# Attention, then eight experts on one core: a few steps of the hand-over moved, and the experts' order table written anew

## The chip, the cores and the metric

The kernel runs on one core of a Trainium2 chip. The metric is the device time of one execution in microseconds (us). The runs of the kernel before gave 601.39, 601.55 and 603.48 us; the median, 601.55 us, is what the change is held against.

## What is computed

The first half is attention in two steps for 8 batches, 8 heads, 576 tokens: 32 packed queries `p` attend to `k` and `v`, and the tokens' queries `q` attend to the 32 packed rows. Its result `x` (4608 x 512) goes to 8 experts. Each expert takes exactly 576 tokens, in the order of all router logits:

```
p_packed = sm_attn(p, k, v);  x = sm_attn(q, p_packed, p_packed)
order = argsort(-(x @ w_gate).flatten())
for idx in order:                      # token, expert
    if assigned[tok] >= 0 or counts[e] >= cap: continue
    assigned[tok] = e; counts[e] += 1
for e in range(E):
    out[assigned == e] = relu(x[assigned == e] @ w1[e]) @ w2[e]
```

All values are float32. The kernel splits each operand of the expert products into a high part and a low part and multiplies three of the four pairs.

## The kernel before, in words

**Attention** is worked through in 16 groups (half the heads of one batch each). A table, `ORDER` (one list per engine, lines 51 to 96), names every step in the order in which its engine gets it, and `follow` (line 271) issues them so. `x0` to `x4` are five TensorE products per group that make rows of `x` (line 715), `xe0` to `xe4` copy them from PSUM to SBUF (lines 742 and 744), and `x_st` (lines 746 to 752) stores them to `xd` in HBM with three DMAs. Those of the last group, 15, go two by SP's queue and one by ACT's. The same table holds the choice of the first expert's tokens, which no loop searches for: `pick_b` finds the expert and marks its tokens, `which` (`expert(0)`, line 1195) turns the expert's number into an integer, and `slot_a` to `slot_f`, `onehot`, `slot_v` and `list_m` to `list_b` (lines 1229 to 1291) number the marked tokens and make the list of their rows. `slot_a` counts the marked tokens by a TensorE product, `slot_b` copies the count, `slot_c` adds two products, the second of which reads that copy. Nine products with zeros (`warm`) stand behind `slot_c`.

**The experts** follow another table, `PACE` (from line 110 on): 2083 steps in one list, and each engine gets its own steps in the list's order. For expert `k`: `gather.k.c` (POOL, line 1302) fetches its 576 rows from `xd` in five pieces; experts 0 and 1 turn them by TensorE (`xt_p`, line 1335, then `xt_h` on ACT, line 1341, and `xt_l` on VectorE, line 1346), the others by way of HBM and VectorE (`xg_st`, `xg_ld`, `xt_t`, `xs_h`, `xs_l`). `load.k.q.w` fetches quarter `q` of weight 1 or 2 (512 KB, SP's queue, lines 1359 and 1363), `split_h` makes its high part on ACT (line 1368) and `split_l` the low part on POOL (line 1374, four pieces each; VectorE for the two of quarter 0 of expert 0). `f1.k.f.n.i` are TensorE's products for the hidden rows (line 1390; `n` is the half of the tokens, `i` the pair of parts), `h_hi` and `h_lo` (ACT line 1396, VectorE line 1401) empty their PSUM bank, `f2.k.f.t` are the products of the second layer (lines 1410 to 1415), `ev` and `ev_b` empty them, and `scatter` (POOL, line 1446) writes the rows out. A load into a buffer waits for the split that read it before.

Beside expert `k` runs the search for the tokens of expert `k+1` and later: `close`, `build` (lines 1052 to 1086, `build_b` is lines 1065 and 1066), then rounds of `count_a` (ACT, line 1098), `count_v` (VectorE, line 1104), `count_m` (TensorE, lines 1110 and 1111) and `upd`, and at last `slot` and `list` as above. `count_a`, `xt_h`, `h_hi`, `split_h` and `ev` share ACT's queue; `slot_e` (lines 1250 to 1252), `build_b`, `h_lo`, `xt_t` and `xs_l` share VectorE's. Three PSUM banks, in turn, serve `f1` and all the small products.

The first expert starts with 24 products with zeros (`warm.0.i`, line 416), spread over the wait for the first gathers. `held_m` (line 1021), `lim_t` and `lim_m` are small products that the search needs before its first round. Two loads of the first expert are held back (`HELD`, line 1348): ahead of the load, SP issues a 4-byte DMA from the tile that a gather fills (`hold`, line 1355), and so SP's queue waits there until that gather has landed.

Of the kernel before, what the change touches and what calls it, by code (L numbers as in the profile page):

```python
# [108 lines left out]

PACE = '''  # L110
    warm.0.0 lead.0 load.0.0.2 warm.0.1 load.0.0.1 warm.0.2 gather.0.0 warm.0.3 warm.0.4 warm.0.5 load.0.1.1 gather.0.1 held_m.0 lim_t.0 held_b.0 warm.0.6 warm.0.7 gather.0.2 lim_b.0
    warm.0.8 split_h.0.0.2 close_a.1 warm.0.9 close_b.1 lim_m.0 gather.0.3 warm.0.10 build_a.1 lim_c.0 warm.0.11 warm.0.12 warm.0.13 split_h.0.0.1 gather.0.4 warm.0.14 build_b.1
    warm.0.15 warm.0.16 warm.0.17 build_s.1 build_t.1 warm.0.18 build_v.1 warm.0.19 warm.0.20 count_v.1.0 warm.0.21 count_a.1.0 xt_p.0.0 split_l.0.0.1 warm.0.22 xt_h.0.0 load.0.1.2
    count_m.1.0 xt_p.0.1 upd_a.1.0 xt_l.0.0 xt_h.0.1 xt_p.0.2 upd_b.1.0 warm.0.23 xt_l.0.1 xt_h.0.2 f1.0.0.0.0 count_a.1.1 xt_l.0.2 load.0.2.1 f1.0.0.0.1 count_v.1.1 f1.0.0.0.2
    upd_c.1.1 count_m.1.1 xt_p.0.3 h_hi.0.0.0 upd_a.1.1 h_lo.0.0.0 xt_p.0.4 xt_h.0.3 upd_b.1.1 xt_h.0.4 f1.0.1.0.0 xt_l.0.3 count_a.1.2 f1.0.1.0.1 xt_l.0.4 f1.0.1.0.2 upd_c.1.2
    f1.0.0.1.0 count_v.1.2 h_hi.0.1.0 split_h.0.1.1 f1.0.0.1.1 h_lo.0.1.0 split_l.0.0.2 f1.0.0.1.2 count_m.1.2 split_l.0.1.1 f1.0.2.0.0 h_hi.0.0.1 split_h.0.1.2 h_lo.0.0.1 f1.0.2.0.1
    load.0.2.2 upd_a.1.2 f2.0.0.3 upd_b.1.2 upd_c.1.3 count_a.1.3 count_v.1.3 f1.0.1.1.0 build_k.1 f1.0.1.1.1 split_h.0.2.1 split_l.0.1.2 load.0.3.1 f1.0.1.1.2 count_m.1.3 f2.0.0.4
    h_hi.0.1.1 upd_a.1.3 f1.0.2.0.2 upd_b.1.3 h_lo.0.1.1 count_a.1.4 f2.0.0.1 count_v.1.4 upd_c.1.4 f1.0.2.1.0 split_l.0.2.1 split_h.0.2.2 load.0.3.2 count_m.1.4 f2.0.1.4 upd_a.1.4
    upd_b.1.4 f2.0.0.0 h_hi.0.2.0 upd_c.1.5 count_a.1.5 h_lo.0.2.0 f2.0.1.1 count_v.1.5 f1.0.2.1.1 f1.0.3.0.0 split_l.0.2.2 count_m.1.5 f1.0.2.1.2 upd_a.1.5 upd_b.1.5 f2.0.1.3
    count_v.1.6 h_hi.0.2.1 count_a.1.6 h_lo.0.2.1 f2.0.0.2 upd_c.1.6 f1.0.3.1.0 split_h.0.3.1 count_m.1.6 f1.0.3.1.1 upd_a.1.6 upd_b.1.6 f1.0.3.0.1 upd_c.1.7 count_a.1.7 split_l.0.3.1  # L120
    f1.0.3.0.2 count_v.1.7 f2.0.1.2 h_hi.0.3.0 split_h.0.3.2 count_m.1.7 f2.0.1.0 upd_a.1.7 upd_b.1.7 h_lo.0.3.0 f2.0.2.2 count_a.1.8 count_v.1.8 split_l.0.3.2 f1.0.3.1.2 upd_c.1.8
    f1.0.4.0.0 h_hi.0.3.1 count_m.1.8 f1.0.4.0.1 upd_a.1.8 upd_b.1.8 f1.0.4.0.2 h_lo.0.3.1 bound_m.1 f2.0.2.0 h_hi.0.4.0 bound_a.1 bound.1 test_c.1 f2.0.2.1 h_lo.0.4.0 test_m.1
    f1.0.4.1.0 test_t.1 test_k.1 f2.0.3.0 assign.1 f1.0.4.1.1 member.1 expert.1 close_a.2 load.1.0.1 slot_a.1 f1.0.4.1.2 close_b.2 f2.0.3.2 h_hi.0.4.1 slot_b.1 build_a.2 f1.0.5.0.0
    load.1.0.2 slot_c.1 f1.0.5.0.1 load.1.1.1 build_b.2 f2.0.2.3 load.1.1.2 slot_d.1 build_s.2 slot_e.1 build_t.2 f1.0.5.0.2 build_v.2 f2.0.3.3 h_lo.0.4.1 count_a.2.0 slot_f.1 f2.0.2.4
    count_v.2.0 f2.0.3.1 onehot.1 h_hi.0.5.0 split_h.1.0.1 count_m.2.0 f1.0.5.1.0 upd_a.2.0 upd_b.2.0 f2.0.4.2 slot_v.1 count_a.2.1 split_l.1.0.1 f2.0.4.0 h_lo.0.5.0 count_v.2.1
    f1.0.5.1.1 split_h.1.0.2 upd_c.2.1 list_m.1 count_m.2.1 f1.0.5.1.2 list_a.1 upd_a.2.1 split_l.1.0.2 f2.0.4.3 upd_b.2.1 load.1.2.1 h_hi.0.5.1 upd_c.2.2 count_a.2.2 h_lo.0.5.1
    list_s.1 f1.0.6.0.0 count_v.2.2 f2.0.5.0 list_b.1 split_h.1.1.1 count_m.2.2 f2.0.3.4 upd_a.2.2 upd_b.2.2 f1.0.6.0.1 gather.1.0 load.1.2.2 count_v.2.3 count_a.2.3 f1.0.6.1.0
    upd_c.2.3 build_k.2 f1.0.6.0.2 gather.1.1 split_h.1.1.2 f1.0.6.1.1 count_m.2.3 f2.0.4.1 upd_a.2.3 h_hi.0.6.0 split_l.1.1.1 upd_b.2.3 f2.0.5.3 upd_c.2.4 count_a.2.4 h_lo.0.6.0
    f1.0.6.1.2 count_v.2.4 f1.0.7.0.0 h_hi.0.6.1 split_h.1.2.1 count_m.2.4 f1.0.7.0.1 h_lo.0.6.1 upd_a.2.4 f1.0.7.0.2 gather.1.2 upd_b.2.4 load.1.3.1 count_v.2.5 count_a.2.5 f2.0.5.1
    upd_c.2.5 f2.0.4.4 gather.1.3 split_h.1.2.2 f2.0.5.2 count_m.2.5 f1.0.7.1.0 h_hi.0.7.0 gather.1.4 upd_a.2.5 upd_b.2.5 f1.0.7.1.1 h_lo.0.7.0 count_a.2.6 upd_c.2.6 xt_p.1.0  # L130
    count_v.2.6 split_l.1.2.1 f1.0.7.1.2 xt_h.1.0 f2.0.5.4 h_hi.0.7.1 count_m.2.6 f2.0.6.0 upd_a.2.6 h_lo.0.7.1 f2.0.6.2 upd_b.2.6 count_v.2.7 count_a.2.7 f2.0.7.0 xt_l.1.0
    split_l.1.1.2 xt_p.1.1 upd_c.2.7 xt_p.1.2 xt_h.1.1 count_m.2.7 f2.0.6.1 xt_h.1.2 upd_a.2.7 upd_b.2.7 xt_l.1.1 xt_p.1.3 count_a.2.8 f2.0.6.4 upd_c.2.8 load.1.3.2 f2.0.7.4
    count_v.2.8 xt_h.1.3 xt_p.1.4 xt_l.1.2 f2.0.6.3 xt_h.1.4 xt_l.1.3 ev.0.0 count_m.2.8 f2.0.7.1 upd_a.2.8 xt_l.1.4 split_h.1.3.1 scatter.0.0 f1.1.0.0.0 upd_b.2.8 count_v.2.9
    f1.1.0.0.1 count_a.2.9 upd_c.2.9 f1.1.0.1.0 split_l.1.2.2 f1.1.0.1.1 ev.0.4 count_m.2.9 f1.1.0.0.2 upd_a.2.9 upd_b.2.9 f1.1.0.1.2 count_v.2.10 h_hi.1.0.0 count_a.2.10 f2.0.7.3
    h_lo.1.0.0 upd_c.2.10 split_l.1.3.1 f2.0.7.2 ev_b.0 ev.0.3 count_m.2.10 f1.1.1.0.0 h_hi.1.0.1 upd_a.2.10 upd_b.2.10 ev.0.1 f1.1.1.0.1 h_lo.1.0.1 ev.0.2 bound_m.2 f1.1.1.0.2
# [1633 lines left out]
```

## Time and profile before

| what | value |
|---|---|
| median of the runs | 601.55 us |
| the profiled execution's own time | 600.76 us |
| its span, first to last instruction | 599.0 us |
| attention and the first expert's list | 0 to about 140 us |
| first product of the first expert | 149.82 us |
| TensorE busy | 580.4 us (97% of the span) |
| VectorE, ScalarE, GpSimd busy | 399.0, 341.8, 369.1 us |

The span is 1.76 us shorter than the profiled execution's time, which is 0.79 us under the median. Times in the rows count from the span's start. A matmul's end in the profile is modelled; the distance from one start to the next is the better measure of what a product costs. "Idle" before an instruction is the time in which its engine did nothing, and the name behind the arrow is what ended it.

### The profile page before, as it was taken

The page shows a single profiled execution, that of the slowest core. Times are in us where ns is not written, and L with a number is a line of the kernel's source. Part 1 is how long each engine was busy: PE and PEld are TensorE (multiplying, and loading weights), DVE is VectorE, ACT ScalarE, POOL GpSimd, SP SyncE. Part 2 cuts the span into 40 slices and gives each one's busy share as a digit, 9 for nine tenths or more (in the row PEclk, how much of TensorE's full clock was granted, in tenths as well). Part 3 has the DMA queues.
Part 4 walks back from the last instruction along what each step waited for, and adds up shares of the span by engine and source line. Part 5 has one row for each costly group of instructions (what it writes and reads, how often), then busy time and mean ns, then how long its engine had stood idle before and what let it go on. Part 6 is the DMA issues. An engine that isn't in the chain of part 4 may idle for free.

```text
span 599.0 us, 12421 instructions
## 1 busy us (share of the span) xinstructions
PE 580.4 (97%) x4145; PEld 494.3 (83%) x4145; DVE 399.0 (67%) x1438; ACT 341.8 (57%) x873; POOL 369.1 (62%) x617
## 2 busy tenths in 40 slices
PE   7999999997999999999999999999999999999994
PEld 4678888784888888887988888989888899989883
DVE  6999999987868685697588649756954342162110
ACT  4888889873857847656655573674443352342111
POOL 6589898883556768548844783881578467453003
PEclk9999999999999999999999999999999999999998
...
GB/s 291 391 370 261 307 333 231 192 159 225 170 10 242 123 164 208 220 91 166 249 130 113 149 242 131 150 197 182 53 203 210 239 78 196 212 8 80 1 1 84
DMA packets 75307, 105.76 MB, mean 177 GB/s; under 512 B 7124, under 2 KB 54756, under 8 KB 75236
## 3 DMA queue, kind: packets, MB, share of 16 engines
...
q8 instruction: 35, 0.57, 0.4%
q10 hardware_dynamic: 576, 0.34, 0.2%
...
## 4 chain that ended last, share of the span: by engine, by line
PE 87%; DVE 5%; ACT 2%; POOL 2%; issue 1%; DMA 1%; SPq 0%; POOLq 0%; DVEq 0%; ACTq 0%
PE hp L1390 34%; PE y L1410 10%; PE y L1411 10%; PE y L1412 9%; PE s L530 9%; PE xp L715 4%; PE y L1414 3%; PE y L1415 2%; PE pp L589 1%; DMA kl<-in_k_dram 1%; PE tr L574 1%; PE pl L1273 1%; PE px L1335 1%; ACT ja L1098 1%; POOL sb L653 1%
## 5 line engine op out<-in xcount | busy, mean ns | idle before, releaser
L1401 DVE SCALAR_TENSOR_TENSOR h<-hp,h 128x64 fp32r<-128x64 f32 (+3 forms) x192 | 61.8, 352 | 107.4 <-ACT h L1396 106.7
L1396 ACT ACTIVATE h<-hp 128x288 fp32r<-128x288 f32 (+2 forms) x128 | 51.7, 407 | 134.0 <-PE hp L1390 65.9
L1374 POOL TENSOR_TENSOR w1l<-w1s,w1h 128x256 fp32r<-128x256 f32 x124 | 89.7, 754 | 53.4 <-ACT w1h L1368 53.2
L1374 POOL TENSOR_TENSOR w2l<-w2s,w2h 128x256 fp32r<-128x256 f32 x124 | 90.5, 761 | 47.2 <-ACT w2h L1368 47.1
L1410 PE MATMUL y<-w2h,h 128*128 128x512 f32 x256 | 103.8, 406 | 0.0
L1411 PE MATMUL y<-w2l,h 128*128 128x512 f32 x256 | 100.6, 393 | 0.0
L1412 PE MATMUL y<-w2h,h 128*128 128x512 f32 x256 | 100.2, 391 | 0.0
L1390 PE MATMUL hp<-xh,w1h 128*128 128x288 f32 (+2 forms) x512 | 89.7, 298 | 1.0 <-DVE h L1401 0.9
L1390 PE MATMUL hp<-xh,w1l 128*128 128x288 f32 (+2 forms) x512 | 90.1, 299 | 0.0
L1390 PE MATMUL hp<-xl,w1h 128*128 128x288 f32 (+2 forms) x512 | 89.8, 298 | 0.0
L1390 PEld LDWEIGHTS hp<-xh,w1h 128*128 128x128 f32 x512 | 77.8, 188 | 7.4 <-ACT h L1396 1.1
L1446 POOL DMA_INDIRECT out_dram<-xg,gi x40 | 39.3, 983 | 69.7 <-DVE xg L1433 35.7
L1098 ACT ACTIVATE ja<-Vt,nT 128x288 bf16<-128x288 f32 x116 | 62.2, 536 | 32.7 <-DVE nT L1125 24.7
L1390 PEld LDWEIGHTS hp<-xl,w1h 128*128 128x128 f32 x512 | 76.4, 188 | 3.5 <-DVE xl L1346 0.2
L1390 PEld LDWEIGHTS hp<-xh,w1l 128*128 128x128 f32 x512 | 76.0, 188 | 2.9
L1412 PEld LDWEIGHTS y<-w2h,h 128*128 128x128 f32 x256 | 48.1, 188 | 10.8
L1302 POOL DMA_INDIRECT xg<-xd,gi x40 | 38.2, 955 | 23.1 <-issue 9.2
L1410 PEld LDWEIGHTS y<-w2h,h 128*128 128x128 f32 x256 | 48.1, 188 | 4.8
L1411 PEld LDWEIGHTS y<-w2l,h 128*128 128x128 f32 x256 | 48.2, 188 | 4.5
L1116 DVE SCALAR_TENSOR_TENSOR g<-pc,thr,s4r 128x3 f32<-128x3 f32 x64 | 14.0, 219 | 41.2 <-PE pc L1111 40.9
L1368 ACT CAST w2h<-w2s 128x1024 fp32r<-128x1024 f32 x32 | 33.3, 1042 | 13.1 <-DMA w2s<-in_moe_w_dram 6.7
L715 PE MATMUL xp<-P,th 128*128 128x264 f32 (+2 forms) x160 | 38.2, 328 | 0.7 <-DVE xs L742 0.3
...
## 6 DMA issues: line engine op xcount, KB each, us to landing
w2s<-in_moe_w_dram SPq DMA_DIRECT2D x32, 512.0 KB, 3.7
w1s<-in_moe_w_dram SPq DMA_DIRECT2D x32, 512.0 KB, 4.4
...
```

Source lines behind the costliest of these rows:

```text
L530: nc.tensor.matmul(t[:, 224 + 9 * a:224 + 9 * b], w[:, db].rearrange("p a b -> p (a b)"), x[:, :, db, a:b].rearrange("p b (t y) -> p t b y ...
L715: nc.tensor.matmul(xp[:m, :n], T[a, g][:, o:o + m], T[w, g][:, :n], start=i == 0, stop=i == 2)
L1098: nc.scalar.activation(ja, Vf, AF.Sign, bias=S_['nT'][:, j:j + 1], scale=-1.0, accum_out=cp[:, j:j + 1])
L1302: nc.gpsimd.indirect_dma_start(out=X['xg', k, c][:m], out_offset=None, in_=xd, in_offset=bass.IndirectOffsetOnAxis(ap=X['gi', k][:m, c:c + ...
L1374: eng.tensor_sub(X[n + 'l', k, q][r], X[n + 's', k, q][r], X[n + 'h', k, q][r].bitcast(F32))
L1390: nc.tensor.matmul(X['hp', k, f, n], X[W, k, q][:, d, 128 * r:128 * r + 128], X[Z, k][:, d, cut(k) * n:576 * n + cut(k) * (1 - n)], start= ...
L1396: nc.scalar.activation(X['h', k, f][:, cut(k) * n:576 * n + cut(k) * (1 - n)], X['hp', k, f, n], AF.Relu)
L1401: V.scalar_tensor_tensor(h[:, o:o + b - a], p[:, a - t * n:b - t * n], 0.0, h[:, a:b].bitcast(F32), op0=OP.max, op1=OP.subtract)
L1410: nc.tensor.matmul(y, hh, wh, start=f == 0, stop=False)
L1411: nc.tensor.matmul(y, hh, wl, start=False, stop=False)
L1412: nc.tensor.matmul(y, hl, wh, start=False, stop=f == 7)
L1446: s = nc.gpsimd.indirect_dma_start(out=out, out_offset=bass.IndirectOffsetOnAxis(ap=X['gi', k][:m, t:t + 1], axis=0), in_=X['yo', k, t][:m ...
```

## The change

Five edits of the code. `slot_a` moves ahead of `x4.15`, the last product of `x`. `which` moves from ACT to VectorE, behind `pick_b`. The third store of group 15 goes by ACT's queue, not SP's. The first expert's load (quarter 1, weight 1) is held until gather 1 has landed; before, it was the one behind it. `PACE` is a new list of the same 2083 steps.

```diff
 ORDER 'ACT':  -  keep_c xe4.14 xe0.15 xe1.15 xe2.15 xe3.15 xe4.15 which
               +  keep_c xe4.14 xe0.15 xe1.15 xe2.15 xe3.15 xe4.15
 ORDER 'DVE':  -  ... choice2 choice3 pick_b slot_b held_a slot_d ...
               +  ... choice2 choice3 pick_b which slot_b held_a slot_d ...
 ORDER 'PE':   -  x3.15 x4.15 slot_a slot_c warm list_m list_s
               +  x3.15 slot_a x4.15 slot_c warm list_m list_s
 PACE = '''
-    warm.0.0 lead.0 load.0.0.2 warm.0.1 load.0.0.1 warm.0.2 gather.0.0 warm.0.3 warm.0.4 warm.0.5 load.0.1.1 gather.0.1 held_m.0 lim_t.0 held_b.0 ...
+    warm.0.0 lead.0 load.0.0.2 warm.0.1 load.0.0.1 warm.0.2 warm.0.3 warm.0.4 held_m.0 warm.0.5 held_b.0 lim_t.0 warm.0.6 gather.0.0 ...
...
     def x_st(g):
...
         for i in range(2):
             q = nc.scalar if g == 15 and i else nc.sync
             q.dma_start(...)
-        nc.sync.dma_start(bass.AP(tensor=xd.tensor, ...), xs[lanes(g, 4), 4, :256])
+        q.dma_start(bass.AP(tensor=xd.tensor, ...), xs[lanes(g, 4), 4, :256])
...
-                ... ('which', 'ACT', .2, lambda: expert(0, nc.scalar), [('pick_b',)]),
+                ... ('which', 'DVE', .2, lambda: expert(0), [('pick_b',)]),
...
-    HELD = {(0, 1, 2): 1, (0, 2, 1): 4}
+    HELD = {(0, 1, 1): 1, (0, 2, 1): 4}
```

A line is one further down in the changed kernel, from the tables on. Three places are shown.

TensorE, end of attention. L715 are the products of `x` (here `x4.15`, three of them), L1231 is `slot_a`, L1239 and L1240 are `slot_c`. Before:

```order
L715 MATMUL xp<-P_2170,th 128x256
L715 MATMUL xp<-P_2301,th 128x256
L715 MATMUL xp<-P_2170,tl 128x256
L1231 LDWEIGHTS mb
L1231 MATMUL psl<-one,mb 36x1
L1239 LDWEIGHTS tri
L1239 MATMUL psl_2429<-mb,tri 128x36
L1240 LDWEIGHTS cs
L1240 MATMUL psl_2429<-tri,cs 128x36
```

Now:

```order
L1232 LDWEIGHTS mb
L1232 MATMUL psl<-one,mb 36x1
L716 MATMUL xp<-P_2170,th 128x256
L716 MATMUL xp<-P_2301,th 128x256
L716 MATMUL xp<-P_2170,tl 128x256
L1240 LDWEIGHTS tri
L1240 MATMUL psl_2429<-mb,tri 128x36
L1241 LDWEIGHTS cs
L1241 MATMUL psl_2429<-tri,cs 128x36
```

`slot_a` stands ahead of `x4.15`'s three products, `slot_c` behind them as before. Not shown, in the new table: five products with zeros instead of six stand ahead of `held_m`, and two stand between the transposes `xt_p.0.1` and `xt_p.0.2`, which followed each other. On ACT, `split_h.0.1.1` now comes ahead of `h_hi.0.1.0` and `count_a.1.2`.

SP's queue from the last store on. L752 (now L753) is the third store, the TENSOR_LOAD reads the first expert's number into a register, w2s and w1s are loads of weights, `hold` is the 4-byte DMA. Before:

```order
L752 DMA xd<-xs 64x256
L1352 TENSOR_LOAD ei
L1352 ISA x2
L1363 ISA
L1363 DMA w2s<-in_moe_w_dram 128x2x512
L1359 ISA
L1359 DMA w1s<-in_moe_w_dram 128x4x256
L1359 ISA
L1359 DMA w1s<-in_moe_w_dram 128x4x256
L1355 DMA hold<-xg 1x1
L1363 ISA
L1363 DMA w2s<-in_moe_w_dram 128x2x512
```

Now:

```order
L752 DMA xd<-xs 64x4x256
L1353 TENSOR_LOAD ei
L1353 ISA x2
L1364 ISA
L1364 DMA w2s<-in_moe_w_dram 128x2x512
L1360 ISA
L1360 DMA w1s<-in_moe_w_dram 128x4x256
L1356 DMA hold<-xg 1x1
L1360 ISA
L1360 DMA w1s<-in_moe_w_dram 128x4x256
L1364 ISA
L1364 DMA w2s<-in_moe_w_dram 128x2x512
```

The third store is gone from this queue, and `hold` stands ahead of the third load instead of the fourth.

POOL, boundary of experts 1 and 2, from the second scatter of expert 1 on. The DMAs to out_dram are scatters of expert 1, L1374 (now L1375) are low parts of weights: w2l is `split_l.2.3.2`, w1l is `split_l.2.3.1`. Before:

```order
L1445 MEMSET spc 1x1
L1446 DMA out_dram<-xg,gi 4608x512
L1374 TENSOR_TENSOR w2l<-w2s,w2h 128x256 x4
L1445 MEMSET spc 1x1
L1446 DMA out_dram<-xg,gi 4608x512
L1445 MEMSET spc 1x1
L1446 DMA out_dram<-xg,gi 4608x512
L1445 MEMSET spc 1x1
L1446 DMA out_dram<-xg,gi 4608x512
L1374 TENSOR_TENSOR w1l<-w1s,w1h 128x256 x4
```

Now:

```order
L1446 MEMSET spc 1x1
L1447 DMA out_dram<-xg,gi 4608x512
L1446 MEMSET spc 1x1
L1447 DMA out_dram<-xg,gi 4608x512
L1446 MEMSET spc 1x1
L1447 DMA out_dram<-xg,gi 4608x512
L1446 MEMSET spc 1x1
L1447 DMA out_dram<-xg,gi 4608x512
L1375 TENSOR_TENSOR w2l<-w2s,w2h 128x256 x4
L1375 TENSOR_TENSOR w1l<-w1s,w1h 128x256 x4
```

`split_l.2.3.2` moves from behind the second of the five scatters to behind all of them. In the table, `slot_e.3` and `build_b.4` stand ahead of it now. At the next boundary `split_l.3.3.2` moves the other way, ahead of all scatters of expert 2, and `slot_e.4` stands 25 steps behind it rather than right behind it.

## Rows read from the trace of the kernel before

**Rows 1.** The page, head and part 1: busy time, share of the span, instructions

```profile
span 599.0 us, 12421 instructions
PE 580.4 (97%) x4145; PEld 494.3 (83%) x4145; DVE 399.0 (67%) x1438; ACT 341.8 (57%) x873; POOL 369.1 (62%) x617
```

**Rows 2.** Windows, PE: stretch, length, PE busy, clock, DMA share, GB/s

```profile
254.00:308.00 54.00, 53.02 (x347) 1.00 0.57 167
308.00:362.00 54.00, 53.16 (x337) 1.00 0.58 164
362.00:416.00 54.00, 54.00 (x348) 1.00 0.54 169
```

**Rows 3.** Timeline, PE, hand-over: start, duration, engine, line, operation, [idle <-releaser]

```profile
134.46 0.44 PE L715 MATMUL xp<-P,th 128*128 128x256 f32 x2
...
134.95 0.18 PE L1231 MATMUL psl<-one,mb 128*36 128x1 bf16 x1
135.06 0.19 PE L1239 MATMUL psl<-mb,tri 128*128 128x36 bf16 x1
135.37 0.19 PE L1240 MATMUL psl<-tri,cs 36*128 36x36 bf16 x1
...
140.14 1.47 PE L416 MATMUL y<-wz 128*128 128x512 bf16 x6 [0.27 <-DVE lt L1290]
...
149.82 0.74 PE L1390 MATMUL hp<-xh,w1h 128*128 128x256 f32 x4
...
151.67 0.16 PE L1110 MATMUL pc<-cp,same 128*128 128x3 f16 x1
```

**Rows 4.** Timeline, DVE, hand-over: the copy of the slot count

```profile
135.16 0.15 DVE L1235 CAST cs<-psl 36x1 bf16<-36x1 f32 x1 [0.88 <-PE psl L1231]
```

**Rows 5.** Timeline, ACT, hand-over

```profile
147.07 0.54 ACT L1098 ACTIVATE ja<-Vt,st 128x288 bf16<-128x288 f32 x1 [1.93 <-issue]
...
149.19 1.07 ACT L1341 CAST xh<-px 128x512 fp32r<-128x512 f32 x2 [0.35 <-PE px L1335]
150.15 0.54 ACT L1098 ACTIVATE ja<-Vt,nT 128x288 bf16<-128x288 f32 x1
...
152.46 0.86 ACT L1341 CAST xh<-px 128x512 fp32r<-128x512 f32 x2 [0.28 <-PE px L1335]
```

**Rows 6.** Timeline, SP's queue, hand-over: start and length of each issue

```profile
135.73 0.56 SPq L752 DMA_DIRECT2D xd<-xs  x1
138.20 0.41 SPq L1363 DMA_DIRECT2D w2s<-in_moe_w_dram  x1
...
147.66 0.77 SPq L1355 DMA_DIRECT2D hold<-xg  x1
148.67 0.40 SPq L1363 DMA_DIRECT2D w2s<-in_moe_w_dram  x1
```

**Rows 7.** Instructions of line 1302 (all 40 gathers): issue to landing

```profile
DMA to landing us min/median/max: 3.0/4.0/5.8
```

**Rows 8.** The page, part 6: DMA issues, count, size, us to landing

```profile
w1s<-in_moe_w_dram SPq DMA_DIRECT2D x32, 512.0 KB, 4.4
```

**Rows 9.** Instructions of line 1065: duration min/median/max in ns, first and last start

```profile
L1065 DVE TENSOR_SCALAR wm<-eq x6: 300/307/1417, 145.2 to 369.7; 128x288 f32<-128x288 f32 x6
```

**Rows 10.** Timeline, DVE, two expert boundaries

```profile
268.33 1.42 DVE L1065 TENSOR_SCALAR wm<-eq 128x288 f32<-128x288 f32 x1
...
324.21 0.78 DVE L1251 TENSOR_SCALAR s2i<-sl 128x36 int32<-128x36 int32 x1
```

**Rows 11.** Timeline, POOL, the same two boundaries

```profile
268.75 3.22 POOL L1374 TENSOR_TENSOR w2l<-w2s,w2h 128x256 fp32r<-128x256 f32 x4
...
323.50 2.81 POOL L1374 TENSOR_TENSOR w2l<-w2s,w2h 128x256 fp32r<-128x256 f32 x4
```

**Rows 12.** Timeline, PE, the same two boundaries

```profile
272.60 0.77 PE L1390 MATMUL hp<-xh,w1h 128*128 128x288 f32 x4 [0.92 <-DVE h L1401]
...
327.62 0.16 PE L1110 MATMUL pc<-cp,same 128*128 128x3 f16 x1 [0.67 <-ACT ja L1098]
```

More of the change, by code (lines that the diff above doesn't have):

```diff
@@ L183 @@
-    xs_h.4.0 f1.3.7.0.0 test_k.5 xs_h.4.1 xs_l.4.0 f2.3.5.1 assign.5 f1.3.6.1.2 member.5 expert.5 test_t.5 load.5.0.1 xt_t.4.2 f2.3.4.0 h_hi.3.6.1 slot_a.5 close_a.6 f1.3.7.0.1
-    xs_h.4.2 close_b.6 f1.3.7.0.2 load.5.0.2 slot_b.5 build_a.6 f2.3.5.0 h_hi.3.7.0 f2.3.5.3 xs_l.4.2 f2.3.5.4 h_lo.3.6.1 f2.3.5.2 build_b.6 split_h.4.3.2 slot_c.5 h_lo.3.7.0 f2.3.6.0
-    xs_l.4.1 slot_d.5 f1.3.7.1.0 split_h.4.3.1 build_s.6 split_l.4.3.2 xt_t.4.3 f2.3.6.1 slot_e.5 xs_h.4.3 f1.3.7.1.1 xt_t.4.4 f1.3.7.1.2 xs_l.4.3 build_t.6 f1.4.0.0.0 h_hi.3.7.1
@@ new lines @@
+    f2.0.1.4 upd_a.1.8 upd_b.1.8 f1.0.3.1.2 bound_m.1 f1.0.4.0.0 h_hi.0.3.1 bound_a.1 test_c.1 f1.0.4.0.1 h_lo.0.3.1 test_m.1 f1.0.4.0.2 test_t.1 test_k.1 f2.0.2.1 bound.1 h_hi.0.4.0
+    assign.1 f1.0.4.1.0 expert.1 member.1 load.1.0.2 close_a.2 f1.0.4.1.1 close_b.2 load.1.0.1 f1.0.4.1.2 build_a.2 slot_a.1 f2.0.2.4 h_hi.0.4.1 f2.0.2.3 load.1.1.2 slot_b.1 build_b.2
+    f2.0.3.1 load.1.1.1 h_lo.0.4.0 build_t.2 f2.0.3.3 build_s.2 build_v.2 h_lo.0.4.1 count_a.2.0 slot_c.1 count_v.2.0 f1.0.5.0.0 slot_d.1 f2.0.3.0 slot_e.1 slot_f.1 split_h.1.0.1
@@ new lines @@
+    scatter.0.2 test_t.2 close_b.3 f1.1.2.0.2 h_lo.1.1.1 slot_a.2 f2.1.0.0 h_hi.1.2.0 load.2.0.2 slot_b.2 build_a.3 scatter.0.3 slot_c.2 load.2.1.1 f2.1.0.4 slot_d.2 f1.1.2.1.0
+    slot_e.2 f1.1.2.1.1 slot_f.2 f1.1.2.1.2 build_b.3 f2.1.0.3 h_hi.1.2.1 slot_v.2 split_h.1.3.2 f2.1.0.1 build_s.3 onehot.2 build_t.3 split_h.2.0.1 f2.1.1.4 split_l.1.3.2 build_v.3
+    f2.1.1.3 h_lo.1.2.1 count_a.3.0 count_v.3.0 list_m.2 h_lo.1.2.0 f1.1.3.1.0 list_a.2 count_m.3.0 f2.1.0.2 upd_a.3.0 upd_b.3.0 load.2.1.2 list_s.2 upd_c.3.1 count_a.3.1 f1.1.3.1.1
@@ new lines @@
+    xs_h.3.2 h_lo.2.6.1 slot_a.4 f2.2.5.4 xs_l.3.2 f1.2.7.0.1 xs_l.3.1 f1.2.7.0.2 close_b.5 f1.2.7.1.0 h_hi.2.7.0 split_h.3.3.1 f1.2.7.1.1 h_lo.2.7.0 build_a.5 f2.2.6.1 f2.2.5.2
+    slot_b.4 build_b.5 split_h.3.3.2 f2.2.6.3 xt_t.3.3 build_t.5 slot_c.4 split_l.3.3.2 f1.2.7.1.2 build_s.5 build_v.5 f2.2.6.2 h_hi.2.7.1 count_v.5.0 xs_h.3.3 slot_d.4 f1.3.0.0.0
+    h_lo.2.7.1 count_a.5.0 xt_t.3.4 f2.2.6.0 f1.3.0.0.1 xs_l.3.3 load.4.1.2 f1.3.0.0.2 xt_t.3.5 f2.2.6.4 h_hi.3.0.0 count_m.5.0 xs_h.3.4 f2.2.7.4 upd_a.5.0 slot_e.4 xs_h.3.5 f2.2.7.3
@@ new lines @@
+    h_hi.4.7.1 split_l.5.3.2 f1.5.1.0.1 h_lo.4.7.1 f2.4.6.2 xs_l.5.4 xs_l.5.5 f1.5.1.0.2 f2.4.6.4 member.7 list_m.6 split_l.5.3.1 f2.4.6.0 load.6.1.2 f1.5.0.1.0 h_hi.5.1.0
+    split_h.6.0.1 f1.5.0.1.1 h_lo.5.1.0 expert.7 f2.4.7.1 slot_a.7 f1.5.0.1.2 split_l.6.0.1 slot_b.7 load.6.1.1 list_a.6 f2.4.7.2 h_hi.5.0.1 h_lo.5.0.1 f2.4.7.0 ev.4.2 close_a.8 ev.4.1
+    f1.5.2.0.0 ev.4.0 f1.5.1.1.0 scatter.4.1 f2.4.7.4 load.6.2.1 f1.5.1.1.1 ev.4.4 slot_c.7 scatter.4.2 f1.5.1.1.2 slot_d.7 slot_e.7 f1.5.2.0.1 h_hi.5.1.1 f2.4.7.3 h_lo.5.1.1 ev_b.4
```

244 lines of the change are left out of this document (117 added, 127 removed).

## The prediction

> **What bounds the kernel now.** First the page's busy shares: TensorE is busy 580.4 of 599.0 us, VectorE, the next, 399.0 [rows 1]. So the change adds or saves time only where TensorE waits. Then the windows: in the stages of the experts TensorE does nothing for 0.98 us between 254 and 308 us and 0.84 us between 308 and 362, and for 0.00 between 362 and 416 [rows 2]. What is left lies in the start, the end, and the hand-over from attention to the first expert at 135 to 150 us. The change has a part for the hand-over (four edits and the head of the new table) and one for the experts (the rest of the table), so I price these two.
>
> **The hand-over, what is before.** The slot count ends a wait of VectorE: its copy starts at 135.16, after 0.88 us idle [rows 4]. `slot_a` ran at 134.95, behind `x4.15` at 134.46 [rows 3]. From there the list goes to the first gathers and the search for expert 1 starts; its first counts on ACT start at 147.07 [rows 5], and behind them on ACT stand the copies of the gathered rows, so the first expert's products begin at 149.82 [rows 3]. The gathers themselves land in 3.0 to 5.8 us, 4.0 in the middle [rows 7]; the second of them had landed at 147.66, when `hold` went out [rows 6]. ACT's copies of the two pieces come after the counts, to 150.26, so the gathers are not what ends last there.
>
> **Slot count ahead of the last product.** `slot_a` takes the place of `x4.15`: 134.46 for 134.95, 0.49 us earlier, and the count is copied as much earlier. But its reader is the second product of `slot_c`, and the first one still stands behind `x4.15`, which ends where `slot_a` ended: it stays at 135.06. Before, the second waited for the copy until 135.37; now it follows at once, 0.11 later as 135.06 follows 134.95, so at 135.17 [rows 3]. Gain for the list: 0.20 us, not 0.49.
>
> **First expert's number by VectorE.** One short instruction is added to VectorE ahead of `slot_b`; the copy of the slot count, about as small, takes 0.15 us [rows 4]. It falls into the 0.88 us idle, of which 0.39 are left once the count comes 0.49 earlier. Cost nothing; without that cover it would be 0.15. ACT loses an instruction at a time when it only waits.
>
> **Third store of group 15 on ACT's queue.** SP's queue is free 0.56 us sooner, plus the 0.12 between the stores, so the first weights go out at about 137.5, not 138.20 [rows 6]. ACT has no work until those weights land. Nothing on the path depends on it, so zero.
>
> **Warm products.** Six products with zeros take 1.47 us, 0.24 each [rows 3]; one less stands ahead of `held_m`, for which VectorE waits. With the 0.20 the search's first counts start 0.44 us earlier, at 146.63 instead of 147.07. I trace what comes of it. The transposes of pieces 1 and 2 stand on TensorE behind the counts' product; before, they followed each other, now two products with zeros stand between, 0.48 us. So the second transpose ends 0.04 us later than before, ACT's copy of it too, and the second round of counts, which stands behind that copy on ACT, starts at 150.2 instead of 150.15 [rows 5]. TensorE meets that round at 151.67 [rows 3], and that time stays. The 0.44 us are given back at the second round.
>
> **Two quarters of weights ahead of the gathers.** The third load (512 KB) now waits for gather 1. The gathers meet less traffic, but they did not end last, so this gains nothing. The price to look for is a late load. Gather 1 landed at 147.66 at the latest, and the load after `hold` went out 1.0 us later, at 148.67 [rows 6]; a load of this kind takes 4.4 us in the middle [rows 8], so it lands by 153.1. Its cast on ACT now stands behind `xt_h.0.4`, which ends at 153.32 [rows 5]. It just fits; if the gathers come earlier, with room. The same for `hold`: behind it on SP are only loads of this expert.
>
> Hand-over in all: 0.0. Ends: -0.44 (nothing given back) and +0.5 (a load late by half a microsecond with ACT's queue behind it).
>
> **The experts' table.** It neither adds nor removes a step, so it can only move TensorE's waits. The two waits are on the boundaries of experts 1 to 2 and 2 to 3: the first until VectorE had emptied a bank, 0.92 us idle, the second until ACT had counted, 0.67 [rows 12]; the windows put them at 0.98 and 0.84 with what belongs to them [rows 2]. Both have one cause. At 268.33 an instruction of `build_b` took 1.42 us on VectorE, though the middle of its six is 0.307 [rows 9, 10]; POOL was at the low part of a quarter of weights, 3.22 us from 268.75 [rows 11]. At 324.21 one of `slot_e` took 0.78 us [rows 10] beside the low part that began at 323.50 [rows 11]. VectorE's queue was late from there, and TensorE behind it.
>
> The Trainium skill (SBUF — State Buffer, section "SBUF: two separate sides") says that VectorE and GpSimd share one pair of ports as an exclusive lock: a VectorE instruction in a two-port mode, or with two inputs in SBUF, and a GpSimd one that reads SBUF wait for each other for the whole instruction. The two stretched rows agree with it. It speaks against a gain: a new order moves such meetings and does not end them, and by it alone the table would be worth zero.
>
> In the new table these two meetings are gone: `slot_e.3` and `build_b.4` come before `split_l.2.3.2`, and `slot_e.4` comes 25 steps behind `split_l.3.3.2`. That is worth 0.98 + 0.84 = 1.82 us. New ones arise, the nearest `build_b.6` beside `split_l.4.2.2` at the boundary of experts 3 to 4. The third window has such a boundary without loss, the two others lost 0.9 each [rows 2]; I take +0.5 for the new ones, with the ends 0 and +1.82 (as many as before).
>
> **Sum.** 600.76 (the profiled execution's own time) + 0.0 - 1.82 + 0.5 = 599.4. It lies 0.79 under the median, and the change is measured against the median: 601.55 - 1.3 = 600.2 us.
>
> **The rivals.**
> *Everything kept.* The hand-over's 0.44 is not given back and no new meeting costs anything: 601.55 - 0.44 - 1.82 = 599.3. For it: ACT idles 1.93 us before the first counts, so its queue has slack [rows 5]. Against it: the two warm products between the transposes.
> *Slower by new meetings of VectorE and POOL.* The rule quoted above is this one. If the low part of `split_l.4.2.2` begins before `build_b.6` is over, `build_b` is late by up to 1.1 us (1.42 against 0.307), and the transposing product behind it with all of TensorE's queue waits; if the two old waits turn up at new places as well, the table costs one more boundary: +0.9, so 602.5. It decides at the start of POOL's low part against the end of `build_b`. For it: VectorE is still 67% busy and POOL 62% [rows 1]. Against it: the third window, which has such a boundary and no loss [rows 2].
> *The table does not do what it says.* POOL's low parts start when weights land and casts end, and the waits stay though the order changes: 601.5.
>
> **Chances.** Forecast 0.48, everything kept 0.17, slower 0.20, no effect 0.15. What a measurement of this kernel can tell from no change is about 0.5%, 3.0 us: under 598.5 or over 604.6. All gains that I can name are 2.26 us, so faster by that takes a favourable run, or idle time that I have not seen, beside the second case: 0.12. Slower by that takes the third case at three boundaries or a load that comes late: 0.08. Within 0.5%: 0.80. The range takes in the second and the third case and the spread of the runs below the median (the profiled execution was 0.79 under it): 598.5 to 603.0 us.
>
> **What would show it.** Right: `slot_a` near 134.5, the second product of `slot_c` near 135.2, first counts near 146.6, the second round's product still near 151.6; no idle of TensorE over 0.3 us at the boundaries of experts 1 to 2 and 2 to 3, `slot_e` and `build_b` there at their short durations. Wrong: TensorE waiting for ACT's cast of the third load after 153 us; an idle time at the boundary of 3 to 4 or another with a stretched VectorE instruction beside a low part; or a first product of the second layer that comes over 0.3 us sooner, which would mean that the hand-over keeps its gain.

## The result, and the profile after

| | median of the runs, us | lowest to highest | profiled execution: time, span |
|---|---|---|---|
| before | 602.18 | 601.39 to 604.10 | 600.76, 599.0 |
| the change | 606.91 | 605.17 to 608.18 | 606.2, 604.4 |

The ratio is 1.0071 with a 95% interval of 1.0049 to 1.0093: slower by 4.7 us, outside the range that the prediction gave and on the side to which it gave a chance of 0.08.

The two profiled spans differ by 5.4 us. Told by the starts of the first and the last product of the experts (149.82 and 590.21 before, 151.41 and 595.98 after), the experts' stage is 4.18 us longer, everything ahead of it 1.59, and the end behind it 0.37 shorter. Of the 1.59, 0.95 stand already at an early product of attention, ahead of any step that was moved (line 530, now 531: 9.79 before, 10.74 after; in four profiles of kernels with the old start, told of below, the same product stands at 9.40 to 10.99).

So the experts first. The head and part 1 of the page of the changed kernel, which answer to [rows 1]:

```profile
span 604.4 us, 12419 instructions
PE 583.9 (97%) x4143; PEld 498.2 (82%) x4145; DVE 399.3 (66%) x1439; ACT 342.0 (57%) x872; POOL 369.1 (61%) x617
```

The busy sums hardly moved; TensorE's grew by 3.5 us for the same products. The windows of TensorE, the first two of which answer to [rows 2] (stretch, length, busy, granted clock, DMA share, GB/s):

```profile
254.00:308.00 54.00, 49.51 (x308) 0.94 0.51 152
308.00:362.00 54.00, 54.00 (x355) 1.00 0.58 164
275.00:278.00 3.00, 2.34 (x17) 1.00 0.28 77
278.00:281.00 3.00, 0.00 (x0) 0.75 0.45 172
281.00:284.00 3.00, 2.17 (x14) 0.50 0.54 171
284.00:287.00 3.00, 3.00 (x22) 0.61 0.05 15
131.00:138.00 7.00, 6.60 (x65) 0.76 0.42 134
```

The 0.84 us of the second window are gone, as forecast. The first window lost 0.98 us before and loses 4.49 now, and its clock is 0.94. The narrow windows place both: TensorE does nothing from 277.3 to 281.8, and while it stands the granted clock falls from 1.00 to 0.50, which is 1.2 GHz for 2.4, where it stays to about 286.3 (0.61 over the last of these windows). The timeline of TensorE there, with the hand-over's products that answer to [rows 3] ahead of it (start, duration, engine, line, operation, idle before and its releaser):

```profile
136.62 0.18 PE L1232 MATMUL psl<-one,mb 128*36 128x1 bf16 x1
...
137.32 0.19 PE L1241 MATMUL psl<-tri,cs 36*128 36x36 bf16 x1
...
151.41 0.70 PE L1391 MATMUL hp<-xh,w1h 128*128 128x256 f32 x4
...
276.65 0.69 PE L1391 MATMUL hp<-xh,w1l 128*128 128x288 f32 x4
281.83 1.24 PE L1274 MATMUL pl<-Bv,A 128*128 128x144 bf16 x9 [4.49 <-DVE g L1117]
282.81 1.31 PE L1391 MATMUL hp<-xh,w1h 128*128 128x288 f32 x4
```

The product that waits is `list_m.3`, the first of the list of expert 3's rows. VectorE at the same time:

```profile
274.90 6.74 DVE L1264 TENSOR_TENSOR Bv<-hr,pv 128x648 bf16<-128x648 bf16 x2
281.57 0.20 DVE L1117 SCALAR_TENSOR_TENSOR g<-pc,thr,s4r 128x3 f32<-128x3 f32 x1
```

And all sixteen instructions that make `Bv` in this program (duration in ns, least, middle and most):

```profile
L1264 DVE TENSOR_TENSOR Bv<-hr,pv x16: 478/489/6331, 139.4 to 457.0; 128x648 bf16<-128x648 bf16 x16
```

One of the sixteen, the first of `slot_v.3`, took 6.33 us instead of 0.49. POOL beside it:

```profile
274.45 0.90 POOL L1447 DMA_INDIRECT out_dram<-xg,gi  x1 [0.32 <-DVE xg L1434]
275.38 2.78 POOL L1375 TENSOR_TENSOR w2l<-w2s,w2h 128x256 fp32r<-128x256 f32 x4
278.13 2.75 POOL L1375 TENSOR_TENSOR w1l<-w1s,w1h 128x256 fp32r<-128x256 f32 x4
```

These are the two low parts that the new table puts behind all scatters of expert 1, eight pieces without a pause from 275.38 to 280.88. `Bv` had begun 0.48 us ahead of the row and ended 0.35 behind it. Behind it in VectorE's queue stands `g` (of `upd_a.4`), which reads, and so frees, the PSUM bank that `list_m.3` is to write; TensorE's whole queue stands behind `list_m.3`. In the kernel before, `Bv` of expert 3 ran at 273.90, beside the issue of a scatter, and the two low parts lay at 268.75 [rows 11] and 276.01, with three scatters between them:

```profile
273.90 0.90 DVE L1263 TENSOR_TENSOR Bv<-hr,pv 128x648 bf16<-128x648 bf16 x2
```

What it costs: from the last start ahead of the hole to the start of `list_m.3` it is 4.79 us, where two starts there are usually 0.13 apart, so 4.66 us are lost. Then products at half clock: the nine of the list take 0.98 us by their starts and the twelve behind them 3.04 (282.81 to 285.85, where the next group starts).

### The profile page after: what moved, and what is told of

Read it like the earlier page. It is cut to its first block, busy times and chain, and to the rows that moved or that the text cites. A ratio compares the mean times of both kernels' runs of the same rounds, so it can differ in the third digit from the quotient of the medians.

```text
span 604.4 us, 12419 instructions
## 1 busy us (share of the span) xinstructions
PE 583.9 (97%) x4143; PEld 498.2 (82%) x4145; DVE 399.3 (66%) x1439; ACT 342.0 (57%) x872; POOL 369.1 (61%) x617
## 3 DMA queue, kind: packets, MB, share of 16 engines
q0 software_dynamic: 5920, 18.88, 9.6%
## 4 chain that ended last, share of the span: by engine, by line
PE 88%; DVE 5%; ACT 2%; POOL 2%; issue 1%; DMA 1%; POOLq 0%; ACTq 0%; DVEq 0%
PE hp L1391 33%; PE y L1411 11%; PE y L1412 10%; PE y L1413 10%; PE s L531 9%; PE xp L716 4%; PE y L1415 3%; PE y L1416 2%; PE pp L590 1%; DVE Bv L1264 1%; PE pl L1274 1%; PE tr L575 1%; PE s L540 1%; DMA pl<-in_p_dram 1%; POOL sb L654 1%
## 5 line engine op out<-in xcount | busy, mean ns | idle before, releaser
L1375 POOL TENSOR_TENSOR w2l<-w2s,w2h 128x256 fp32r<-128x256 f32 x124 | 89.9, 757 | 68.9 <-ACT w2h L1369 68.7
L1375 POOL TENSOR_TENSOR w1l<-w1s,w1h 128x256 fp32r<-128x256 f32 x124 | 89.6, 756 | 39.1 <-ACT w1h L1369 39.0
```

The lines of the kernel that those rows point to most:

```text
L1375: eng.tensor_sub(X[n + 'l', k, q][r], X[n + 's', k, q][r], X[n + 'h', k, q][r].bitcast(F32))
```

## The experiments

Four theories. **P**: `Bv` of expert 3 meets POOL's row; the wait and the half clock behind it are the loss. **H**: the loss is in the hand-over. **L**: the list's product stands too early in TensorE's order, and would wait whatever VectorE does. **A** (formed later): whether `Bv` is held depends on how far ahead of the row it starts.

The runs went to several chips, and the kernel before itself differs between them: 602.16 us (median of 20 runs) where e9 to e12 ran, as in the first runs, but 612.75, 611.81 and 617.97 (one run) where e1 to e4, e5 to e8, and e13 and e14 ran. Every ratio is to the kernel before on the same chip. Expected times in us, where they were given on the first chip's level, are held against that ratio.

### Is it the meeting? `Bv` moved away from the row (e1, e12, with the change itself as e9)

```diff
 PACE of the change
-  ... onehot.3 build_t.4 ...   ... h_hi.2.1.1 slot_v.3 count_m.4.0 ...
+  ... onehot.3 slot_v.3 build_t.4 ...   ... h_hi.2.1.1 count_m.4.0 ...
```

> The changed kernel with one step of the table moved: the two products of the list of expert 3 (slot_v.3, the line of Bv) stand on VectorE right behind onehot.3, some 1.8 us earlier, so that they are over before GpSimd begins its eight pieces of split_l.2.3.2 and split_l.2.3.1. Theory P (the loss is the meeting of that VectorE step with GpSimd's unbroken run of eight pieces): the 5.84 us by which Bv is stretched, TensorE's wait of 4.66 us ahead of the list's products, and the half clock behind it (some 2.1 us: nine list products 0.98 instead of 0.54, twelve of f1 3.04 instead of 1.60) go together: 606.9 - 6.7 = about 600.2 us, no half clock between 275 and 290. Rival H (the loss is in the hand-over: half clock from 133 to 136, first product of the experts at 151.41 instead of 149.82, fewer weights ahead): stays within 0.5 us of 606.9. Rival L (the list's products stand too early on TensorE, and would wait there for VectorE in any case): the wait shrinks by 1 to 2 us only, about 605.

Measured: 607.23 us, ratio 0.9915 (0.9889 to 0.9942); `Bv` took 0.92 us, and there was no hole. The same kernel was run again beside the change where the kernel before takes 602:

> The changed kernel as it is, beside the three runs of this call: the stretched Bv (6.33 us) and the hole of 4.66 us in TensorE near 275 to 280, half clock behind it. Ratio to before 1.000 if this chip is like that of e5 (signals of TensorE up to 1.2 us late at some dozen places), 1.007 if it is like that of the first measurement (none late).

Measured: 607.01 us, ratio 1.009 (1.0059 to 1.0121), the same hole of 4.66 us, stage 445.01.

> e1's kernel again (slot_v.3 behind onehot.3), now beside the changed kernel on one chip: theory P: 5 to 6.7 us under it, no Bv over 0.6 us, no half clock between 275 and 290; against before the ratio of e1, 0.991 (0.989 to 0.994), on a chip with late signals, or about 0.997 on one without.

Measured: 600.02 us, ratio 0.9951 (0.9929 to 0.9973), 7.0 us under e9 and faster than both kernels. Its stage takes 438.81 us, 440.77 before (both to the end of the last product). VectorE, then POOL, then TensorE, then the window of TensorE of e12:

```profile
273.33 0.92 DVE L1264 TENSOR_TENSOR Bv<-hr,pv 128x648 bf16<-128x648 bf16 x2
```

```profile
276.46 2.80 POOL L1375 TENSOR_TENSOR w2l<-w2s,w2h 128x256 fp32r<-128x256 f32 x4
```

```profile
277.86 0.74 PE L1274 MATMUL pl<-Bv,A 128*128 128x144 bf16 x9
278.39 0.77 PE L1391 MATMUL hp<-xh,w1h 128*128 128x288 f32 x4
...
280.07 0.36 PE L1286 MATMUL plw<-ld,rep 128*128 128x18 bf16 x8
```

```profile
254.00:308.00 54.00, 53.71 (x350) 1.00 0.59 176
```

The row is the same eight pieces (the second four follow at 279.23), the list's product stands in the same place in TensorE's order, and it does not wait: P holds, L falls. The list's nine products and the twelve behind them take 0.53 and 1.68 us here, 0.98 and 3.04 at half clock, so the slow clock cost 1.8 us on these alone. The 6.20 us between the two stages (445.01 and 438.81) are the hole, 4.66, and the slow products, 1.8, less a new wait of about 0.3 (TensorE idle 0.29 ahead of 276.14).

### Is it the table? (e3, e7, e5, e6)

e3 puts the new table alone into the kernel before:

```diff
 the kernel before
-PACE = (the table before)
+PACE = (the table of the change)
```

> The kernel before with the new experts' table alone: slot_a behind x4.15, which on ScalarE, the third store by SyncE and three weight quarters ahead of the gathers stay as they were. Theory P: all of the loss is the table's, 606 to 607.5 us, with the same stretched Bv and hole near 275. Rival H (the loss is the four small edits' at the hand-over): the two waits of before (0.98 and 0.84 us) go and nothing comes, about 600.4.

Measured: 611.34 us, ratio 0.9978 (0.9951 to 1.0006). VectorE, then TensorE of e3:

```profile
274.07 6.77 DVE L1263 TENSOR_TENSOR Bv<-hr,pv 128x648 bf16<-128x648 bf16 x2
```

```profile
281.03 1.06 PE L1273 MATMUL pl<-Bv,A 128*128 128x144 bf16 x9 [4.52 <-DVE g L1116]
```

The hole is the table's: no other edit is in this kernel. That it is not slower than the kernel before was a miss; on this chip that kernel loses time elsewhere (last section). e7 is the reverse, the four other edits with the old table:

```diff
 the change
-PACE = (the table of the change)
+PACE = (the table before, load.0.1.1 moved to just ahead of load.0.1.2)
```

> The changed kernel with the old experts' table (load.0.1.1 moved behind the first gathers in it, so that still only two weight quarters go ahead of the gathers): the four small edits alone. Theory P: they are worth nothing, ratio to before 0.999 to 1.002. Rival H: they carry the loss, 1.004 to 1.008, and the first product of the experts comes later against the tally than in the kernel before.

Measured: 610.73 us, ratio 0.9985 (0.9955 to 1.0016): nothing that can be measured, so H falls. e5 and e6 are the change and the kernel before themselves, on the chip of e7 (e3 ran on another one, where the kernel before is as slow):

> The changed kernel as it is, on the chip of these experiments, whose kernel before takes 612.75 us instead of 602.18, so that the runs e1 to e4 have something of their own chip to stand against. Theory P (the meeting of Bv with eight pieces of split_l, as a wait and as half clock): 607.2 of e1 with 6.7 us more, about 614, or above e2's 615.4 by the clock's 2 us, about 617; the ratio to before 1.002 to 1.008. Rival H (hand-over): the table alone took 611.3 here, so the change is that and the hand-over's loss, 614 to 616. The two part in the profile: P wants the stretched Bv, the hole near 275 to 280 and half clock behind it, and a hand-over (from the first product of the tally to the first product of the experts, 19.3 us before) within 0.6 us; H wants a hand-over longer by 2 us or more.

Measured: 611.97 us, ratio 0.9998 (0.9975 to 1.0022), with `Bv` held for 6.33 us and the hole of 4.66.

> The kernel before as it is, for its profile on the chip of these experiments: ratio 1.00, and the place of the 10 us by which this chip is slower than the one of the first measurement. If they lie in waits of TensorE for count_a within the experts' stage (as e1 to e4 have some that the first profiles had not), this chip gives back less of what the new table saves and the hole has to be read by its own rows; if they lie ahead of the experts, only the sum is larger.

Measured: 612.39 us, ratio 1.0007 (0.9981 to 1.0034), stage 451.2 us where the first profile has 440.8.

### Is it the length of the row? (e8, e4)

e8 splits the row: the second four pieces go behind a gather.

```diff
 PACE of the change
-  ... upd_c.4.1 split_l.2.3.1 load.3.1.2 ...   ... gather.3.3 f2.2.0.0 ...
+  ... upd_c.4.1 load.3.1.2 ...   ... gather.3.3 split_l.2.3.1 f2.2.0.0 ...
```

> The changed kernel with split_l.2.3.1 moved on GpSimd behind the first gather of expert 3, so that four pieces stand in a row where Bv meets them, not eight. Theory P: Bv is held for about 3.1 us instead of 5.84 (as A at 452.51, beside four pieces: 3.18), the hole in TensorE shrinks from 4.66 to about 1.9 us, and the half clock may stay away: 2.8 to 4.9 us under the changed kernel of this call. If the length of the row doesn't matter (Bv waits for something else, as the scatters' issue): no change within 0.5 us.

Measured: 606.41 us, ratio 0.9896 (0.9842 to 0.9949), 5.6 us under e5 on the same chip, more than expected; in the two profiles the experts' stage is 3.8 us shorter (445.3 for 449.1, between starts) and the hand-over 1.1. VectorE, POOL and TensorE of e8:

```profile
275.84 4.03 DVE L1264 TENSOR_TENSOR Bv<-hr,pv 128x648 bf16<-128x648 bf16 x2
```

```profile
276.32 2.78 POOL L1375 TENSOR_TENSOR w2l<-w2s,w2h 128x256 fp32r<-128x256 f32 x4
```

```profile
280.06 0.72 PE L1274 MATMUL pl<-Bv,A 128*128 128x144 bf16 x9 [1.78 <-DVE g L1117]
280.58 0.77 PE L1391 MATMUL hp<-xh,w1h 128*128 128x288 f32 x4
```

`Bv` is held beside four pieces too, but its first instruction only for 3.13 us; TensorE's hole is 1.94, and the products behind it run at full clock. So the held time is the rest of the row, and it was the shift behind all scatters, which closed two rows into one, that made the wait as long as it is. e4 shifts only `split_l.2.3.2` behind the third scatter, in the kernel before:

```diff
 PACE of the kernel before
-  ... f2.1.6.0 split_l.2.3.2 h_hi.2.0.1 ...   ... scatter.1.2 f1.2.2.0.0 ...
+  ... f2.1.6.0 h_hi.2.0.1 ...   ... scatter.1.2 split_l.2.3.2 f1.2.2.0.0 ...
```

> The kernel before with one step of its old table moved: split_l.2.3.2 on GpSimd behind the five scatters of expert 1 instead of between the second and the third, so that eight pieces of split_l stand in an unbroken row as in the changed kernel. Theory P: the row runs from about 272.6 to 278.1, a list step of expert 3 on VectorE (bf16: hr, Bv or A, from 272.9 on) is held until its end, the list's products, due at 276.8, wait until about 280, and the clock may fall: -1.0 for the old wait, +3 to +5 for the hole and the clock, 604 to 606 us. Rival H and rival L: the old wait of 0.98 us goes and nothing comes, about 601.2.

Measured: 611.37 us, ratio 0.9976 (0.9947 to 1.0005). A miss: the row of eight came, but later. VectorE and POOL of e4:

```profile
278.05 0.90 DVE L1263 TENSOR_TENSOR Bv<-hr,pv 128x648 bf16<-128x648 bf16 x2
```

```profile
280.69 2.81 POOL L1374 TENSOR_TENSOR w2l<-w2s,w2h 128x256 fp32r<-128x256 f32 x4
```

`Bv` was through 1.7 us ahead of it. A long row alone costs nothing; what stands beside it on VectorE decides.

### What is the clock's share? (e2, e11)

Both put twenty products with zeros, which nothing reads, ahead of `list_m.3`, so that TensorE works through the hole. In e2 they go into the list's own bank:

```diff
     def list_m():
         p = S_['pl'] = bank("pl")
+        if S_['nl'] == 4: keep_warm(nc, p, wz, 20)
```

> The changed kernel with 20 added products of zeros in TensorE's queue right ahead of the list's products of expert 3, in the bank that these then overwrite (about 0.235 us each, 4.7 us in all): TensorE works through the hole instead of standing still, and nothing else is changed. Theory P says that the meeting costs twice, once as a wait of 4.66 us, which stays, and once as the half clock behind it, some 2.1 us by the rows, which should go: 606.9 - 2.1 = about 604.8 us, granted clock 1.00 from 281 to 287. If the clock's share is nothing by itself (it only slows work that has slack): 606.9. Rival H: 606.9, or more by what the zeros overshoot.

Measured: 615.4 us, ratio 1.0054 (1.002 to 1.0088). A miss, and the most telling one: TensorE of e2:

```profile
284.48 6.04 PE L417 MATMUL pl<-wz 128*128 128x512 bf16 x20 [4.49 <-DVE g L1117]
```

The zeros read nothing of `Bv`, and yet waited the same 4.49 us. So it is the bank that waits for VectorE, not the list's operands alone. e11 puts them into a bank that is free:

```diff
     def list_m():
+        if S_['nl'] == 4: keep_warm(nc, PL['ps'].tile([128, 512], F32, name="y1"), wz, 20)
         p = S_['pl'] = bank("pl")
```

> The changed kernel with 20 products of zeros ahead of the list's products of expert 3 as in e2, but into the bank of y1, which is free from the scatter of expert 1 until f2.2.0.1, and not into the bank that TensorE has to wait for: in e2 the zeros themselves waited 4.49 us for VectorE's g, which stands behind Bv, and came on top. Here they fill the hole (20 x 0.235 = 4.7 us against 4.66). If the half clock behind the hole costs by itself (2.1 us by the rows): 2 us under the changed kernel of this call, granted clock 1.00 from 280 to 290. If the following products have slack for it: no change.

Measured: 605.28 us, ratio 1.0059 (1.0028 to 1.0089). TensorE of e11, then the windows of all engines of e11 and of e9 (busy of TensorE, its weight loads, VectorE, ACT, POOL; then the clock):

```profile
277.88 4.26 PE L417 MATMUL y<-wz 128*128 128x512 bf16 x19
282.31 0.72 PE L1277 MATMUL pl<-Bv,A 128*128 128x144 bf16 x9 [0.16 <-DVE g L1117]
282.84 0.77 PE L1394 MATMUL hp<-xh,w1h 128*128 128x288 f32 x4
```

```profile
282.00:284.00 2.00, 1.84 (x19) 1.69 (x18) 1.97 (x13) 1.05 (x3) 0.00 (x0) 1.00 0.58 175
```

```profile
282.00:284.00 2.00, 1.81 (x12) 1.80 (x12) 1.57 (x10) 1.17 (x4) 0.00 (x0) 0.50 0.63 187
```

With TensorE busy through the wait the clock stays at 1.00, and the same products take their short times. The medians differ by 1.73 us, of the size of the 1.8 above, but that shows little: the two intervals overlap, and the profiled execution of e11 (608.21 us) has a stage 1.55 us longer than e9's. In it another VectorE instruction with two inputs in SBUF is held beside POOL's next row of eight (from 291.99 to 297.57), `ck` of `build_k`, 3.55 us for 0.46; TensorE then waits 1.79 us, and its clock is at 0.50 for 3.41 us from 300.97. VectorE, then TensorE of e11:

```profile
294.34 3.55 DVE L1071 TENSOR_TENSOR ck<-eq,k 128x288 f32<-128x288 f32 x1
```

```profile
300.23 0.16 PE L1111 MATMUL pc<-cp,same 128*128 128x3 f16 x1 [1.79 <-ACT ja L1099]
```

In e9 the same `ck` took 0.78 us, and nothing waited. So the share of the clock rests on the products' own times.

### Does the lead decide? (e10, e13, e14)

Each delays one instruction of VectorE by writing a tile that nothing reads, to shift it against POOL's row. e10 and e13 do so ahead of `Bv`, once and three times, in the change; e14 once ahead of `A` of expert 4 (`onehot`), which in the kernel before stands beside a row too and passes.

```diff
     def slot_v():        # e10; e13: three times; e14: the same in onehot, kernel before
         S_['Bv'] = small([128, 9, 2, 18, 4], "Bv", BF)
+        if S_['nv'] == 4: V.memset(small([128, 64], "pad"), 0.0)
```

> The changed kernel with one clearing of an unused 128x64 tile (about 0.1 us) on VectorE right ahead of the two Bv products of expert 3, so that Bv begins 0.1 us later against GpSimd's row of split_l. In the traces so far a list step that began 0.48 to 0.51 us ahead of the row was held to the row's end (Bv at 274.90, A at 446.91 and 452.51, the same in all runs), one that began 0.38 or 0.59 to 0.62 ahead of it lost only 0.33 to 0.57 us (A at 275.63 and 332.02 of the kernel before). Theory P as stated (whoever meets the row waits for its end): Bv is held about 5.7 us, time within 0.5 us of the changed kernel of this call. Rival A (the hold hangs on the tenth of a microsecond): Bv begins 0.38 ahead, is held under 0.6 us, the hole goes, and one instruction more makes the kernel about 5 us faster.

Measured: 605.46 us, ratio 1.0073 (1.0045 to 1.0101); the lead is 0.41 us, for 0.48, TensorE's hole is the same 4.49 us, and `Bv` (VectorE, then POOL, of e10) is still held. The time is 1.5 us under e9, more than the 0.5 expected; in the profiles 1.1 of it lies in the hand-over, where e9 has half clock and e10 has not.

```profile
273.95 6.67 DVE L1267 TENSOR_TENSOR Bv<-hr,pv 128x648 bf16<-128x648 bf16 x2
```

```profile
274.35 2.79 POOL L1378 TENSOR_TENSOR w2l<-w2s,w2h 128x256 fp32r<-128x256 f32 x4
```

> The changed kernel with three clearings of the unused tile ahead of Bv of expert 3 (the one of e10 moved Bv's start from 0.48 to 0.41 us ahead of the row, and it was held 5.77 us all the same): Bv begins about 0.3 us ahead of the row. If the lead decides, it is no longer held to the end (A of expert 3 in the kernel before passed with a lead of 0.38): hole gone, some 5 to 7 us under the changed kernel. If not the lead but the place does (any start under the last scatter's issue loses to the row): held about 5.7 us, hole of 4.6 us, no change.

Measured, one run: 614.37 us beside 617.97 of the kernel before (one run too, so the times say little); the lead is 0.04 us, the first instruction of `Bv` takes 5.91, and TensorE's hole is 4.52.

> The kernel before with one such clearing ahead of A of expert 4 (332.02 there, a lead of 0.59 to 0.62 us on a row of four pieces, passed with 0.55): the lead becomes about 0.5, the one at which Bv of expert 3 and A of expert 6 were held. If the lead decides, A is held about 3.2 us to the row's end and TensorE gets a wait of some 2 us near 335; if the place does, it passes with some 0.55 as without the clearing.

Measured, one run: 612.41 us beside 617.97; the lead is 0.54 us, and `A` passes with 1.24 us, 0.49 over its usual time. VectorE, then POOL, of e14:

```profile
339.08 1.24 DVE L1270 TENSOR_TENSOR A<-sbf,iob 128x1152 bf16<-128x1152 bf16 x1
```

```profile
339.62 3.36 POOL L1377 TENSOR_TENSOR w1l<-w1s,w1h 128x256 fp32r<-128x256 f32 x4
```

A falls as a rule: `Bv` is held at leads of 0.04, 0.41 and 0.48 us, and `A` passes at 0.54 here and at 0.38 in the kernel before (275.63, with the row from 276.01, in 1.08 us), but is held at 0.50 (446.91, below). Where `A` passes, POOL pays: the row of four takes 3.36 us here and 3.37 there, for 2.8.

Not the lead, but what POOL does when the VectorE instruction starts, parts the records of all 16 traces. Of the `A` and `Bv` instructions of the experts that began up to their own usual length ahead of a row, 32 began while POOL issued a scatter and the row stood right behind that issue: all 32 lost, 8 of them 0.33 to 0.57 us, and 24 the rest of the row. The other 44 began while POOL was idle, and none lost over 0.02 us, at leads of 0.02 to 0.48. One of these, `A` of e3, 0.07 us ahead of a row of eight (VectorE, then POOL's first four pieces):

```profile
183.16 0.75 DVE L1267 TENSOR_TENSOR A<-sbf,iob 128x1152 bf16<-128x1152 bf16 x1
```

```profile
183.23 3.37 POOL L1374 TENSOR_TENSOR w1l<-w1s,w1h 128x256 fp32r<-128x256 f32 x4 [10.66 <-ACT w1h L1368]
```

A scatter's issue without a row behind it does no such harm: `Bv` of e12 began under one (273.33) and took its 0.92 us. The expectation of e13 names this place, but no run takes the scatter away and leaves the rest, so it is a regularity of the records and not a shown cause. `ck` of e11, which began inside a row, is outside it. What lets 8 pass and holds 24 stays open.

## Why the prediction was wrong

**What bounds the kernel** was right as far as it goes: time came and went where TensorE waits, and also in the products just behind a wait, for which the prediction had no term.

**Slot count ahead of the last product.** Right in its steps: `slot_c`'s second product follows `slot_a` by 0.70 us (136.62 to 137.32); the forecast was 0.71 (134.46 to 135.17), and before it was 0.42 [rows 3].

**The hand-over's sum**, 0.0, was of the right size, with one wrong step. The 0.44 us were not given back at the second round: from the tally of the first expert (the first product of `tally`) to the first expert's first product it was 19.34 us before, and 18.88 and 18.87 in e10 and e11, and the first product of the second layer follows 7.3 to 7.4 us behind in all of them. Where TensorE's clock is at 0.50 for a part of 131 to 138 us (0.76 over that window in the changed kernel's profile), this gain is lost: 19.89. That happened in 5 of the 16 profiles, e4's among them, whose hand-over is the old one. e7 says what the four edits are worth in all: nothing that can be measured.

**Two quarters of weights ahead of the gathers.** Right; ACT of the changed kernel:

```profile
154.13 0.86 ACT L1342 CAST xh<-px 128x512 fp32r<-128x512 f32 x2 [0.47 <-PE px L1336]
154.88 1.06 ACT L1369 CAST w1h<-w1s 128x1024 fp32r<-128x1024 f32 x1
```

The held load was issued at 149.21 and landed at 153.47 (4.26 us; 4.4 was taken), and its cast follows `xt_h` at once.

**The two waits of the table** were right: both are gone, and e12, in which no long wait takes their place, has a stage 1.96 us shorter than before, where 1.82 were forecast. That the two are so close is in part luck: TensorE's idle time in the stage fell by 1.32 us (1.81 to 0.49), and 0.6 of the 1.96 lies in no wait that the records show.

**New meetings of VectorE and POOL, +0.5: the step that failed.** The mechanism was the rival's own. But the prediction looked for it at another place (`build_b.6`, boundary of experts 3 to 4), and sized it by the longer of the two meetings that it had read, an instruction of 1.42 us for 0.307. The trace of the kernel before has a larger one, which the prediction does not name and for which TensorE did not wait: `A` at 446.91, held to the end of a row of four (VectorE, then POOL):

```profile
446.91 3.94 DVE L1267 TENSOR_TENSOR A<-sbf,iob 128x1152 bf16<-128x1152 bf16 x1
```

```profile
447.41 2.81 POOL L1374 TENSOR_TENSOR w1l<-w1s,w1h 128x256 fp32r<-128x256 f32 x4
```

The order of POOL's queue, shown ahead of the prediction, had the cause in it: two low parts of 2.8 us each next to each other. I read this as a move of one of them away from `build_b` and did not ask what stands beside the pair. Three sizes were missing: the held time is the rest of the row, 5.84 us beside eight pieces and 3.13 beside four (3.62 for 0.49, e8), not about 1.1; VectorE's queue behind the held instruction frees a PSUM bank, so all of TensorE's queue stands, 4.66 us; and a stop of that length is paid again by products at 1.2 GHz, 1.8 us. Together 6.5, less the 1.8 gained, is +4.7; the stage measured +4.18, so about half a microsecond is not accounted for.

The Trainium skill (SBUF — State Buffer, section "SBUF: two separate sides") has the pair of ports as an exclusive lock that whichever instruction starts first keeps for its whole length. By it `Bv`, with two inputs in SBUF, would wait for one piece of about 0.7 us at most, and only if the piece began first. The trace agrees that the two exclude each other, and differs in the rest: by the records `Bv` began 0.48 us ahead of the row and got nothing until all eight pieces were through. The row of `build_b` that the prediction counted as agreeing differs in the same way: it began at 268.33, ahead of the low part's 268.75, and still took 1.42 us [rows 10, 11]. The measurement decides here.
